# Attention scores kept in DRAM by pairs of heads, in place of a stage of whole tiles in SBUF

## The chip, the cores and the metric

The kernel runs as one program on 1 core of one Trainium2 chip. The metric is device time in microseconds (us). The kernel before takes 1350.86 us (median of 3 runs, 1349.09 to 1351.36).

## The reference

Three layers in float32. The change touches the first alone, an attention whose heads are mixed before and after the softmax:

```python
scores = scale * q @ k.T                                  # 4 batches, 12 heads, 448 queries x 448 keys, D = 64
scores = einsum('bhij,hg->bgij', scores, w_pre)           # mix the heads
attn = softmax(scores, axis=-1)
attn = einsum('bhij,hg->bgij', attn, w_post)              # mix them again
x = (attn @ v)                                            # to [1792, 768]
x = relu(x @ w_in) ** 2 @ w_out                           # feed-forward, 2048 wide
out = gate * relu(x @ w1[e]) @ w2[e]                      # top-1 of 8 experts per token
```

## The kernel before

A matrix multiply can mix heads only if the heads of a query lie on partitions. The scores come out of TensorE the other way, with queries on partitions and one head after another in the free dimension. So all scores (4 x 12 x 448 x 448 floats, 38.5 MB) are moved by DMA from one layout to the other.

**Scores.** `scores(T, j)` (L189) makes one pair of heads `j` for a tile `T` of queries: 6 matmuls (L196; q and k are split into a high and a low part), and a copy by ScalarE (ACT) into `stage[T % 2]` in SBUF (L197), which holds [queries, 12 heads, 448 keys]. A tile has 110 or 118 queries, four tiles a batch, 16 in all. The host has put the queries of a tile in an order in which every G-th row belongs to one group (L1478 to L1482).

**Groups.** A group is 10 queries, taken as 2 halves of 5; 45 groups a batch. `load(p)` (L317) fills the buffer `sg` for the pair of groups `p`, by four DMAs: L328 reads 5 rows of the stage, 12 heads each, and writes 60 partitions of 448 floats. There are four such buffers.

**A tick.** `tick(p)` (L410) is one step of a pipeline with 90 pairs of groups. Its matmuls are the mix of pair p (L343, 8 instructions in the trace: 4 matmuls of two passes each), the second mix of pair p-3 (L375), and in most ticks a piece of attn @ v (`pv`, L395). VectorE (DVE) takes the maximum (L348) and copies results (L384, L399), ACT the exponentials (L354). `make` runs `scores` when `due()` (L304) says so: after a group has been loaded, a target of finished heads for the next tile is noted (L329, L330). The groups of a tile can be loaded only when all its 12 heads are in the stage, and `do_load` (L440) runs LOAD = 2 pairs ahead of the next one.

**Order.** The order of the instructions on each engine is that of the Python program. All DMAs of this phase are issued by SP's one queue, in order: q and k (L174, L183), v once a batch (L302, 1.5 MB), groups (L328), results xT (L401). A DMA that must wait holds up those behind it. After attention comes the feed-forward layer (from L658), whose first weights are loaded in the last ticks (`ahead`, L444; L520, L523).

Of the kernel before, what the change touches and what calls it, by code (L numbers as in the profile page):

```python
# [8 lines left out]
F32 = mybir.dt.float32  # L9
# [13 lines left out]
ROW = 1792  # L23
# [87 lines left out]
        return self.mem.ring(offs, shape, dt) if n else self.mem.at(offs[0], shape, dt)  # L111


def attention(tc, mem, q, k, v, w_pre, w_post, xT, preload, prefetch):

# [3 lines left out]
    nc = tc.nc  # L121
    B, NT, _, HP, MT = q.shape
    S, D, H = k.shape[-1], v.shape[-1], 2 * HP
    NJ = v.shape[2]
    GI = 5
    GP, GC = GI * H, 64
# [1 line left out]
    HH, HQ = H // 2, HP // 2  # L128
    scale = 1.0 / float(D) ** 0.5
    WARM, KEEP = 10, 1  # L130
    LOAD = 2

    with ExitStack() as ctx:
        lo = Cut(mem, Q0, QR + QT + QW)
# [8 lines left out]
        q_raw, raw1, raw2 = lo([128, HP, MT])(), lo([128, S]), lo([128, S])  # L143
        e0 = Cut(mem, E0, 14 * ROW)
        r = Cut(mem, R0, SB_SIZE - R0)
        stage = [c([MT, H, S])() for c in (r, e0)]
        sgs = [c([128, 2, S]) for c in (e0, r, r)] + [mem.at(Q0 + QR + QT, [128, 2, S])]
        e_tiles = [r([128, 8 * GC]) for _ in range(8)]
        e_r = Ring(e_tiles)
# [6 lines left out]
        pairs = mem.open_pairs(ctx)  # L156
        ps_s, ps_o, ps_m = pairs[0], pairs[3], pairs[1:3]

        tiles, groups = [], []
        for b in range(B):  # L160
            for t in range(NT):
                n = S // NT - S // NT % (2 * GI)
                n = S - t * n if t == NT - 1 else n
                G = -(-n // (2 * GI))
                ms = [min(2 * GI, n - 2 * GI * i) for i in range(G)]
                groups += [(len(tiles), i, m) for i, m in enumerate(ms)]
                tiles.append((b, t, G, max(i + G * (m - 1) for i, m in enumerate(ms)) + 1))
        NG, NP = len(groups), len(tiles) * H
        NK, GB = NG // 2, NG // B

        def q_load(T, half):
            b, t = tiles[T][:2]
            c = slice(half * HQ, (half + 1) * HQ)
            nc.sync.dma_start(out=q_raw[:, c], in_=q[b, t][:, c])  # L174

        def q_split(T, half, copy=None):

            c = slice(half * HQ, (half + 1) * HQ)
            (copy or nc.scalar.copy)(q_hi[:, c], q_raw[:, c])
            nc.gpsimd.tensor_tensor(q_lo[:, c], q_raw[:, c], q_hi[:, c].bitcast(F32), ALU.subtract)  # L180
# [4 lines left out]
        def k_split(j, raw, copy=None, eng=None):  # L185
            (copy or nc.scalar.copy)(k_hi[j], raw)
            (eng or nc.gpsimd).tensor_tensor(k_lo[j], raw, k_hi[j].bitcast(F32), ALU.subtract)

        def scores(T, j, ps=ps_s):  # L189

            M = tiles[T][3]
            ps = ps[:M, :, :S]
            for i, (qs, ks) in enumerate(((q_hi, k_hi), (q_lo, k_hi), (q_hi, k_lo))):
                for n in range(2):
                    p = slice(n * D, (n + 1) * D)
                    nc.tensor.matmul(ps[:, n], qs[p, j, :M], ks[j][p], start=(i == 0), stop=(i == 2))  # L196
            nc.scalar.copy(stage[T % 2][:M, 2 * j:2 * j + 2], ps)  # L197

        pro = Cut(mem, A0, SB_SIZE - A0)
        raws = [pro([128, S])() for _ in range(HP)]  # L200
# [27 lines left out]
        for j in range(HP):  # L228
            if j == 1:
                q_split(0, 1, nc.vector.tensor_copy)  # L230
            k_split(j, raws[j], nc.vector.tensor_copy, nc.gpsimd if j in (1, 3) else nc.vector)
            scores(0, j, (ps_s, ps_o)[j % 2])
            keep(KEEP)
        for half in range(2):
            q_load(1, half)
# [4 lines left out]
        for n, (w, src) in enumerate(zip(ws, (w_pre, w_post))):  # L240
            ps = ps_m[1][:, n, :H]
# [4 lines left out]
                nc.vector.tensor_tensor(wpre[:, :GP].rearrange("p (i g) -> p i g", g=H), blk, wr.unsqueeze(1).to_broadcast([128, GI, H]), ALU.mult)  # L246
            else:
                nc.vector.tensor_tensor(wpost, blk.rearrange("p i h -> p h i"), wr.unsqueeze(2).to_broadcast([128, H, GI]), ALU.mult)

        state = {"made": H, "load": 0, "tick": 0}  # L250

        class Feed:

# [5 lines left out]
            def load(self):  # L259
                n = len(self.loaded)  # L260
                self.items[n][1]()
                self.loaded.append(state["tick"])
# [21 lines left out]
        def k_items():  # L284
            place = lambda n: raws3[n % 3]()
            out = []
            for b in range(B - 1):
                for j in range(HP):
                    n = len(out)
                    out.append((("k", b + 1, j), lambda b=b, j=j, n=n: k_load(b + 1, j, place(n)),  # L290
                                lambda j=j, n=n: k_split(j, place(n)),
                                lambda b=b, j=j: state["made"] > ((b + 1) * NT - 1) * H + 2 * j))
            return out
# [1 line left out]
        q_items = [((T, n), lambda T=T, n=n: q_load(T, n), lambda T=T, n=n: q_split(T, n),  # L295
                    lambda T=T, n=n: state["made"] >= (T - 1) * H + (n + 1) * HH) for T in range(len(tiles)) for n in range(2)]
        ks, qs = Feed(k_items(), 3), Feed(q_items, 2, done=4)
        v_t, a_t, sg_t, soft, targets = {}, {}, {}, {}, []

        def v_load(b):  # L300
            v_t[b] = vs()
            nc.sync.dma_start(out=v_t[b], in_=v[b])  # L302

        def due():  # L304

            return (max([n for t, n in targets if t <= state["tick"]] + [state["made"]]) - state["made"]) // 2

        def make(n):

            while state["made"] < min(n, NP):  # L310
                T, h = divmod(state["made"], H)
                qs.need((T, h // HH))
                ks.need(("k", tiles[T][0], h // 2))
                scores(T, h // 2)
                state["made"] += 2

        def load(p):  # L317

            sg_t[p] = sg = sgs[p % 4 if p < NK - 3 else p - NK + 3]()
            for n in range(2):  # L320
                T, i, m = groups[2 * p + n]
                G = tiles[T][2]
                make((T + 1) * H)
                for half in range(2):
                    c = min(GI, m - half * GI)
                    if c > 0:
                        i0 = i + half * GI * G
                        nc.sync.dma_start(out=sg[n * GC:n * GC + c * H, half], in_=stage[T % 2][i0:i0 + G * (c - 1) + 1:G])  # L328
            pace = 1.6 if T + 2 == len(tiles) else 1.25  # L329
            targets.append((state["tick"] + 1, (T + 1) * H + 2 * min(HP, int(HP * pace * (i + 1) / G + 0.5))))  # L330

        def do_load(n):
            while state["load"] < min(2 * n, NG):
# [12 lines left out]
        def row_max(p):  # L346
            soft[p]["nmx"] = nmx_r()
            nc.vector.tensor_reduce(soft[p]["nmx"], soft[p]["ps"][:, :, :S], AX.X, ALU.max, negate=True)  # L348
# [53 lines left out]

            return out

        adds, todo = [], []

        def put(lag, f):
            adds.append((state["tick"] + lag, f))

        def tick(p):  # L410

            state["tick"] += 1
            n = state["tick"]
            ps, ops = ps_m[p % 2], []
            if due() > 1:
                make(state["made"] + 2)
            if todo:
                u, j = todo.pop(0)
                ops.append(pv(u, j, mem.banks[j % 2] if p >= NK + 3 else ps_s[:, j % 2] if state["made"] == NP else ps[:, 0]))
                if j == HP - 1 and (u + 1) * NU % GB == 0 and (u + 1) * NU // GB + 1 < B:  # L420
                    v_load((u + 1) * NU // GB + 1)
            if 0 <= p - 3 < NK:
                ops.append(post(p - 3))
            if 0 <= p - 1 < NK:
                row_max(p - 1)
                exps(p - 1)
            for op in ops:
                op()
            if 0 <= p - 2 < NK:
                scaled(p - 2)  # L430
            if 0 <= p - 3 < NK and any((g + 1) % NU == 0 for g in (2 * p - 6, 2 * p - 5)):
                todo.extend([((2 * p - 5) // NU if (2 * p - 4) % NU == 0 else (2 * p - 6) // NU, j) for j in range(HP)])
            for x in [x for x in adds if x[0] <= n]:
                adds.remove(x)
                x[1]()
            qs.step()
            ks.step()
            if due():
                make(state["made"] + 2)
            do_load(p + 1 + LOAD)  # L440
            if p < NK:
                soft[p] = {"ps": mix(p, ps)}

        ahead = preload(lambda: state["load"] > NG - tiles[-1][2], lambda: state["load"] == NG)  # L444
        for b in range(2):
            v_load(b)
        do_load(1)
# [18 lines left out]
class Ffn:  # L466
# [137 lines left out]
    def preload(self, room, clear):  # L604

        self.rest = self.first_steps(room, clear)
        return self.rest
# [783 lines left out]
def fused_kernel(ctx: ExitStack, tc: tile.TileContext, q, k, v, w_pre, w_post, w_in, w_out, emb, tau, w1, w2, out):  # L1391
    nc = tc.nc
    PE, SP = mybir.EngineType.PE, mybir.EngineType.SP
    H, S = 2 * k.shape[1], k.shape[-1]
    D = v.shape[-1]
    NT, DM = out.shape
    NS = 22
    dram = ctx.enter_context(tc.tile_pool(name="dram", bufs=1, space=DRAM))
    keep = ctx.enter_context(tc.tile_pool(name="keep", bufs=1))
    xT = dram.tile([H * D, NT], F32, name="xT")  # L1400
# [3 lines left out]
    mem = Memory(tc, ctx, SB_SIZE)  # L1404
    en = dram.tile(emb.shape, F32, name="en")
    rt = Router(tc, keep, mem, emb, tau, NT, NS, ident, en)
    ff = Ffn(tc, mem, xT, w_in, w_out, ident, yrow, rt)
# [23 lines left out]
    ET = mybir.EngineType  # L1431
    with tc.manual_schedule(engines={PE}):
        with tc.manual_schedule(engines={SP, ET.Activation, ET.DVE, ET.Pool}):
            attention(tc, mem, q, k, v, w_pre, w_post, xT, ff.preload, ff.prefetch)
        ff.run(late)
    with tc.manual_schedule(engines={PE, SP}):
        wake = ff.last_step(mem.banks[6])
# [2 lines left out]
        rows = ff.tail(mem.bank_ring(2, 3, 4, 5))  # L1440
# [68 lines left out]
```

## Time and profile before

| | us |
|---|---|
| median of 3 runs | 1350.86 |
| profiled execution, its own time | 1344.71 |
| its span (first to last instruction) | 1343.0 |
| PE busy | 1260.3 |
| DVE busy | 934.4 |
| ACT busy | 807.0 |
| POOL busy | 107.0 |

The engines run side by side, so the busy times do not add up. A busy PE is not PE at its peak, since the ends of its pipelined matmuls are modelled. The page's slices show the DMA engines at 3 to 5 tenths during attention; that is a mean over all 16 of them.

### The profile page before, as it was taken

How to read it: one execution, taken by the hardware profiler on the slowest of the kernel's cores; microseconds unless marked ns; L12 is line 12 of the kernel's file. 1: busy time of each engine (PE TensorE's matmuls, PEld its weight loads, DVE VectorE, ACT ScalarE, POOL GpSimd, SP SyncE). 2: the span in 40 equal slices, each digit the busy share in tenths (PEclk: the TensorE clock that was granted, in tenths of full speed). 3: DMA queues.
4: the chain of work that ended last, by engine and by line, in shares of the span. 5: the costliest groups of instructions: out<-in, count | busy, mean ns of one | idle time of the engine just before them, and what ended most of it. 6: DMA issues, size and time to landing. Idle time of an engine off the chain costs nothing. (4 is left out here: it accounts for less than half of the span.)

```text
span 1343.0 us, 31443 instructions
## 1 busy us (share of the span) xinstructions
PE 1260.3 (94%) x12516; PEld 951.2 (71%) x12516; DVE 934.4 (70%) x1598; ACT 807.0 (60%) x1411; POOL 107.0 (8%) x121
## 2 busy tenths in 40 slices
PE   7899979989998869999999999999999999999997
PEld 2455545545655458777898888888886888888886
DVE  3566546655664559998555743498558999999994
ACT  3656545545654546555566444534457888888884
POOL 2020002002000000000000000000001111111100
PEclk7999989998999889999999999999999999999999
DMA  6344344344434545554101000000624147783240
GB/s 219 119 127 145 114 147 143 123 147 126 131 109 121 182 132 176 184 186 155 45 24 60 24 1 0 24 36 12 246 71 178 36 142 280 286 307 115 77 171 26
DMA packets 81641, 166.13 MB, mean 124 GB/s; under 512 B 7359, under 2 KB 58303, under 8 KB 80848
## 3 DMA queue, kind: packets, MB, share of 16 engines
q1 hardware_dynamic: 78432, 151.41, 33.8%
q0 software_dynamic: 2880, 12.59, 2.6%
q8 instruction: 101, 1.65, 0.5%
q14 instruction: 52, 0.43, 0.1%
q10 hardware_dynamic: 176, 0.05, 0.0%
HBM read 184.44 MB, written 18.11 MB: 151 GB/s over the span
## 5 line engine op out<-in xcount | busy, mean ns | idle before, releaser
L577 ACT CAST t<-t 128x768 fp32r<-128x768 f32 x128 | 106.9, 837 | 188.9 <-PE bank L679 84.2
L578 DVE TENSOR_TENSOR t<-t 128x768 fp32r<-128x768 f32 x128 | 122.0, 955 | 120.0 <-ACT t L577 72.1
L343 PE MATMUL pair<-t 60*64 60x448 f32 x720 | 163.7, 595 | 23.4 <-DMA t<-t 22.8
L348 DVE TENSOR_REDUCE t<-pair 128x2 f32<-128x896 f32 x90 | 98.2, 1091 | 102.8 <-PE pair L343 102.7
L354 ACT ACTIVATE t<-pair,t 128x448 f32<-128x448 f32 x180 | 112.5, 631 | 64.0 <-DVE t L348 63.8
L658 PE MATMUL bank<-t 128*128 128x512 f32 (+1 forms) x384 | 140.1, 373 | 8.3 <-ACT t L577 7.3
L1274 DVE TENSOR_TENSOR t<-t 128x768 fp32r<-128x768 f32 x144 | 134.8, 955 | 14.5 <-PE bank L1332 5.0
L384 DVE COPY t<-pair 128x480 f32<-128x480 f32 x168 | 103.0, 652 | 57.4 <-PE pair L375 56.1
L659 PE MATMUL bank<-t 128*128 128x512 f32 (+1 forms) x384 | 138.7, 370 | 1.0 <-DVE t L592 0.9
L1267 DVE TENSOR_TENSOR t<-t 128x1024 fp32r<-128x1024 f32 x102 | 123.3, 1224 | 18.7 <-ACT t L1266 5.3
L197 ACT COPY t<-pair 110x896 f32<-110x896 f32 (+1 forms) x96 | 86.2, 897 | 74.1 <-PE pair L196 37.1
L1273 ACT CAST t<-t 128x768 fp32r<-128x768 f32 x144 | 117.0, 845 | 18.3 <-PE bank L1327 15.3
L1266 ACT CAST t<-t 128x1024 fp32r<-128x1024 f32 x102 | 105.6, 1053 | 25.4 <-PE bank L1289 21.1
L375 PEld LDWEIGHTS pair<-t 60*64 60x64 f32 x5760 | 100.0, 137 | 27.0 <-issue 20.5
L196 PE MATMUL pair<-t 64*110 64x448 f32 (+1 forms) x576 | 89.2, 416 | 26.9 <-ACT t L197 25.3
L375 PE MATMUL pair<-t 60*64 60x60 f32 x5760 | 111.5, 224 | 2.0 <-ACT t L384 1.4
L343 PEld LDWEIGHTS pair<-t 60*64 60x64 f32 x720 | 37.2, 137 | 100.5 <-DMA t<-t 72.3
L395 PEld LDWEIGHTS pair<-t 128*64 128x64 f32 x1056 | 66.9, 142 | 50.4 <-issue 22.9
L1326 PE MATMUL bank<-t 128*128 128x512 f32 (+1 forms) x288 | 98.2, 344 | 0.8 <-ACT t L1337 0.8
L395 PE MATMUL pair<-t 128*64 128x150 f32 (+1 forms) x1056 | 86.2, 308 | 6.4 <-ACT t L399 5.3
L658 PEld LDWEIGHTS bank<-t 128*128 128x128 f32 x384 | 73.9, 192 | 25.2 <-ACT t L577 11.6
L675 PE MATMUL bank<-t 128*128 128x512 f32 (+1 forms) x384 | 90.1, 369 | 0.6 <-ACT t L399 0.6
(219 smaller groups left out, 2312.4 us busy)
## 6 DMA issues: line engine op xcount, KB each, us to landing
t<-in_moe_w_dram SPq DMA_DIRECT2D x120, 512.0 KB
t<-in_moe_w_dram SPq DMA_DIRECT2D x80, 768.0 KB
t<-t SPq DMA_DIRECT2D x356, 105.0 KB
t<-in_moe_w_in_dram SPq DMA_DIRECT2D x16, 768.0 KB
t<-in_moe_w_out_dram SPq DMA_DIRECT2D x16, 768.0 KB
t<-in_vp_dram SPq DMA_DIRECT2D x4, 1536.0 KB
t<-in_q_dram SPq DMA_DIRECT2D x32, 180.0 KB
t<-in_k_dram SPq DMA_DIRECT2D x24, 224.0 KB
```

What stands on the lines that cost most here:

```text
L343: nc.tensor.matmul(ps[half * GC:(half + 1) * GC, n, :S], wpre[i], sg[i, half], start=True, stop=True)
L354: nc.scalar.activation(out=e[:, :S], in_=d["ps"][:, n, :S], func=AF.Exp, bias=d["nmx"][:, n:n + 1], scale=1.0, accum_out=d["z"][:, n:n + 1])
L375: nc.tensor.matmul(wide[c * GC:(c + 1) * GC, r, n, j], e[i, kc * GC:(kc + 1) * GC], wz[i].rearrange("p g i -> p (g i)"), start=True, stop= ...
L395: nc.tensor.matmul(ps[i * D:(i + 1) * D], v_t[u * NU // GB][:, c, h], a_t[u][:, c, h, :n], start=(c == 0), stop=(c == NJ - 1))
L577: nc.scalar.copy(hi, src)
L578: nc.vector.tensor_tensor(lo, src, hi.bitcast(F32), ALU.subtract)
L658: nc.tensor.matmul(ps, wih[:, c], self.xh[k]()[:, :n], start=(k == 0), stop=False)
L659: nc.tensor.matmul(ps, wih[:, c], self.xl[k]()[:, :n], start=False, stop=False)
L1266: nc.scalar.copy(wh, w)
L1267: nc.vector.tensor_tensor(wl, w, wh.bitcast(F32), ALU.subtract)
L1273: nc.scalar.copy(wh, w)
L1274: nc.vector.tensor_tensor(wl, w, wh.bitcast(F32), ALU.subtract)
```

## The change

The stage in SBUF is gone, and with it the order of the queries that the host made. Each `scores` copies its pair of heads into one of 6 small buffers `st` ([112, 2, 448]), and a DMA (L192) writes it to a DRAM tensor `sd[b]` of shape [448 queries, 12 heads, 448 keys], one tick later. A group is loaded from there by one DMA (L326) of 60 partitions x 2 rows. Tiles are now 112 queries throughout. `due(p)` is a straight line in p with a lead of 3 pairs, and DMAs put off to a later tick are issued at the tick's start.

```diff
-        stage = [c([MT, H, S])() for c in (r, e0)]
+        st_r = e0([MT, 2, S], F32, 6)
+        r.off += 12 * ROW
...
+        sd = [dram.tile([S, H, S], F32, name=f"scores{b}") for b in range(B)]
...
-        def scores(T, j, ps=ps_s):
+        def scores(T, j, ps=ps_s, lag=1):
...
-            nc.scalar.copy(stage[T % 2][:M, 2 * j:2 * j + 2], ps)
+            nc.scalar.copy(st, ps)
+            put(lag, lambda: nc.sync.dma_start(out=sd[b][t * MT:(t + 1) * MT, 2 * j:2 * j + 2], in_=st))
...
-            scores(0, j, (ps_s, ps_o)[j % 2])
+            scores(0, j, (ps_s, ps_o)[j % 2], 0)
...
-        def due():
+        def due(p):
-            return (max([n for t, n in targets if t <= state["tick"]] + [state["made"]]) - state["made"]) // 2
+            return min(NP, int((p + LOAD + LEAD) * 4 * GI * H / MT) + H) - state["made"]
...
-                make((T + 1) * H)
-                for half in range(2):
-                    c = min(GI, m - half * GI)
-                    if c > 0:
-                        i0 = i + half * GI * G
-                        nc.sync.dma_start(out=sg[n * GC:n * GC + c * H, half], in_=stage[T % 2][i0:i0 + G * (c - 1) + 1:G])
-            pace = 1.6 if T + 2 == len(tiles) else 1.25
-            targets.append((state["tick"] + 1, (T + 1) * H + 2 * min(HP, int(HP * pace * (i + 1) / G + 0.5))))
+                b, q0, m = groups[2 * p + n]
+                make((b * NT + -(-(q0 + m) // MT)) * H)
+                i = n * GC
+                if m == 2 * GI:
+                    nc.sync.dma_start(out=sg[i:i + GP], in_=sd[b][q0:q0 + m].rearrange("(u c) h s -> (c h) u s", u=2))
+                else:
+                    for u, c in enumerate((GI, m - GI)):
+                        nc.sync.dma_start(out=sg[i:i + c * H, u], in_=sd[b][q0 + u * GI:q0 + u * GI + c].rearrange("c h s -> (c h) s"))
...
+            for x in [x for x in adds if x[0] <= n]:
+                adds.remove(x)
+                x[1]()
-            if due() > 1:
+            if due(p) > 3:
                 make(state["made"] + 2)
...
-            if due():
+            if due(p) > 1:
                 make(state["made"] + 2)
...
-        ahead = preload(lambda: state["load"] > NG - tiles[-1][2], lambda: state["load"] == NG)
+        ahead = preload(lambda: True, lambda: state["load"] == NG)
```

Three places show what moves. The first is SP at the start of the program, before the first mix (`in_vp` is v, `t<-t` a group from the stage):

```order
L208 DMA t<-in_w_post_dram 12x12
L174 DMA t<-in_q_dram 128x360 x2
L302 DMA t<-in_vp_dram 128x3072 x2
L328 DMA t<-t 60x1x448 x4
L174 DMA t<-in_q_dram 128x360
L183 DMA t<-in_k_dram 128x448
L328 DMA t<-t 60x1x448 x8
```

The same place in the changed program (L211 is L208, L169 is L174, L303 is L302):

```order
L211 DMA t<-in_w_post_dram 12x12
L192 DMA scores_110<-t 112x896 x6
L169 DMA t<-in_q_dram 128x336 x2
L303 DMA t<-in_vp_dram 128x3072 x2
L326 DMA t<-scores_110 60x2x448 x2
L169 DMA t<-in_q_dram 128x336
L178 DMA t<-in_k_dram 128x448
L326 DMA t<-scores_110 60x2x448 x4
```

Six writes of scores, each of which waits for ACT's copy, now stand ahead of the loads of q and v. The second place is SP in the middle of attention, before:

```order
L401 DMA xT<-t 128x150
L174 DMA t<-in_q_dram 128x360
L183 DMA t<-in_k_dram 128x448
L328 DMA t<-t 60x1x448 x4
L401 DMA xT<-t 128x150
L183 DMA t<-in_k_dram 128x448
```

And in the changed program (L400 is L401, L178 is L183):

```order
L400 DMA xT<-t 128x150
L192 DMA scores_111<-t 112x896
L169 DMA t<-in_q_dram 128x336
L178 DMA t<-in_k_dram 128x448
L326 DMA t<-scores_111 60x2x448 x2
L400 DMA xT<-t 128x150
L192 DMA scores_111<-t 112x896
```

Per tick, four loads of a group's half became one write and two loads. The third place is PE, from pair 43 on, before (L343 mix, L395 pv, L375 second mix, L196 scores):

```order
L343 MATMUL pair_113<-t 64x448 x4
L395 MATMUL pair_112<-t 64x150 x8
L375 MATMUL pair_114<-t 64x60 x32
L196 MATMUL pair_111<-t 110x448 x6
L343 MATMUL pair_112<-t 64x448 x4
L196 MATMUL pair_111<-t 110x448 x6
L395 MATMUL pair_113<-t 64x150 x8
L375 MATMUL pair_114<-t 64x60 x32
L196 MATMUL pair_111<-t 110x448 x6
L343 MATMUL pair_113<-t 64x448 x4
```

And in the changed program (L342, L394, L374, L190 in their place):

```order
L342 MATMUL pair_107<-t 64x448 x4
L394 MATMUL pair_108<-t 64x150 x8
L374 MATMUL pair_109<-t 64x60 x32
L190 MATMUL pair_106<-t 112x448 x6
L342 MATMUL pair_108<-t 64x448 x4
L394 MATMUL pair_107<-t 64x150 x8
L374 MATMUL pair_109<-t 64x60 x32
```

The scores came in some ticks twice and in others not at all; now nearly each tick has one set, at its end.

## Rows read from the trace of the kernel before

**Rows 1.** Stretches: us; busy of PE, PEld, DVE, ACT, POOL; PEclk, DMA share, GB/s
```profile
0.00:25.70 25.70, 19.38 (x72) 7.29 (x72) 10.69 (x21) 7.63 (x8) 9.07 (x25) 0.82 0.70 246
25.70:425.20 399.50, 359.40 (x6978) 210.99 (x6978) 234.25 (x523) 219.88 (x526) 47.17 (x46) 0.95 0.41 129
425.20:473.70 48.50, 40.75 (x860) 24.40 (x860) 25.90 (x55) 24.19 (x66) 0.00 (x0) 0.93 0.55 172
473.70:510.00 36.30, 25.44 (x361) 21.03 (x361) 24.45 (x40) 18.71 (x41) 0.00 (x0) 0.86 0.52 156
510.00:1343.00 833.00, 815.28 (x4250) 687.49 (x4248) 639.12 (x961) 536.63 (x772) 50.77 (x50) 0.99 0.32 113
```

**Rows 2.** Waits, 25.7 to 473.7: who <- for what: us, times, longest
```profile
PEld pair L343 <- DMA t<-t: 69.4, 81, 5.7
...
PEld pair L196 <- ACT t L197: 41.1, 25, 7.1
...
ACT t L197 <- DMA t<-t: 31.8, 10, 9.9
...
PE pair L343 <- DMA t<-t: 19.4, 30, 5.3
```

**Rows 3.** Timeline of PE, undisturbed stretch: start, us, engine, line, operation, shapes, count
```profile
316.09 0.98 PE L343 MATMUL pair<-t 60*64 60x448 f32 x8
317.00 1.24 PE L395 MATMUL pair<-t 128*64 128x150 f32 x16
318.17 1.16 PE L375 MATMUL pair<-t 60*64 60x60 f32 x64
319.26 0.87 PE L196 MATMUL pair<-t 64*119 64x448 f32 x6
320.06 0.98 PE L343 MATMUL pair<-t 60*64 60x448 f32 x8
...
324.03 0.98 PE L343 MATMUL pair<-t 60*64 60x448 f32 x8
```

**Rows 4.** DMA, 40 to 78 us: packets by size; queue share; issues, KB each
```profile
DMA packets 2709, 4.36 MB, mean 115 GB/s; under 512 B 229, under 2 KB 2701, under 8 KB 2701
...
q1 hardware_dynamic: 2701, 4.25, 35.4%
...
t<-t SPq DMA_DIRECT2D x33, 105.0 KB
t<-in_q_dram SPq DMA_DIRECT2D x4, 180.0 KB
```

**Rows 5.** DMA, 30 to 430 us: the same columns
```profile
DMA packets 35401, 51.51 MB, mean 129 GB/s; under 512 B 3220, under 2 KB 35072, under 8 KB 35072
...
q1 hardware_dynamic: 35328, 50.46, 40.1%
...
t<-t SPq DMA_DIRECT2D x316, 105.0 KB
```

**Rows 6.** SP issue durations, by line: ns min/median/max, first and last start
```profile
L328 SPq DMA_DIRECT2D t<-t x360: 742/763/2046, 16.4 to 465.9; - x180
...
L401 SPq DMA_DIRECT2D xT<-t x72: 319/608/1285, 81.4 to 505.2; - x72
...
L520 SPq DMA_DIRECT2D t<-in_moe_w_in_dram x16: 378/379/1182, 431.1 to 606.4; - x16
```

**Rows 7.** Timeline of the program start, idle time before and its releaser in brackets
```profile
8.13 0.89 SPq L302 DMA_DIRECT2D t<-in_vp_dram  x2
...
15.42 0.91 ACT L197 COPY t<-pair 110x896 f32<-110x896 f32 x1 [0.22 <-PE pair L196]
...
16.35 3.64 SPq L328 DMA_DIRECT2D t<-t  x4
...
20.43 1.72 PE L343 MATMUL pair<-t 60*64 60x448 f32 x2 [2.97 <-DMA t<-t]
```

**Rows 8.** Waits of the SP queue, 30 to 640 us
```profile
SPq L600 <- DMA t<-xT: 8.2, 2, 4.3
```

More of the change, by code (lines that the diff above doesn't have):

```diff
@@ L111, in __call__, with attention @@
         return self.mem.ring(offs, shape, dt) if n else self.mem.at(offs[0], shape, dt)
-def attention(tc, mem, q, k, v, w_pre, w_post, xT, preload, prefetch):
+def attention(tc, mem, dram, q, k, v, w_pre, w_post, xT, preload, prefetch):
     nc = tc.nc
@@ L130, in attention @@
     WARM, KEEP = 10, 1
-    LOAD = 2
+    LOAD, LEAD = 2, 3
     with ExitStack() as ctx:
@@ L157, in attention @@
         ps_s, ps_o, ps_m = pairs[0], pairs[3], pairs[1:3]
[L159 to L167, printed above, removed]
+        tiles = [(b, t) for b in range(B) for t in range(NT)]
+        groups = [(b, q0, min(2 * GI, S - q0)) for b in range(B) for q0 in range(0, S, 2 * GI)]
+        sd = [dram.tile([S, H, S], F32, name=f"scores{b}") for b in range(B)]
         NG, NP = len(groups), len(tiles) * H
@@ L171, in q_load @@
         def q_load(T, half):
-            b, t = tiles[T][:2]
+            b, t = tiles[T]
             c = slice(half * HQ, (half + 1) * HQ)
@@ L187, in k_split @@
             (eng or nc.gpsimd).tensor_tensor(k_lo[j], raw, k_hi[j].bitcast(F32), ALU.subtract)
-        def scores(T, j, ps=ps_s):
-            M = tiles[T][3]
-            ps = ps[:M, :, :S]
+        def scores(T, j, ps=ps_s, lag=1):
+            ps, st, (b, t) = ps[:MT, :, :S], st_r(), tiles[T]
             for i, (qs, ks) in enumerate(((q_hi, k_hi), (q_lo, k_hi), (q_hi, k_lo))):
@@ L195, in scores, with put @@
                     p = slice(n * D, (n + 1) * D)
-                    nc.tensor.matmul(ps[:, n], qs[p, j, :M], ks[j][p], start=(i == 0), stop=(i == 2))
-            nc.scalar.copy(stage[T % 2][:M, 2 * j:2 * j + 2], ps)
+                    nc.tensor.matmul(ps[:, n], qs[p, j], ks[j][p], start=(i == 0), stop=(i == 2))
+            nc.scalar.copy(st, ps)
+            put(lag, lambda: nc.sync.dma_start(out=sd[b][t * MT:(t + 1) * MT, 2 * j:2 * j + 2], in_=st))
+        state, adds = {"made": H, "load": 0, "tick": 0}, []
+        def put(lag, f):
+            if lag:
+                adds.append((state["tick"] + lag, f))
+            else:
+                f()
         pro = Cut(mem, A0, SB_SIZE - A0)
@@ L248, in attention @@
                 nc.vector.tensor_tensor(wpost, blk.rearrange("p i h -> p h i"), wr.unsqueeze(2).to_broadcast([128, H, GI]), ALU.mult)
-        state = {"made": H, "load": 0, "tick": 0}
         class Feed:
@@ L297, in attention @@
         ks, qs = Feed(k_items(), 3), Feed(q_items, 2, done=4)
-        v_t, a_t, sg_t, soft, targets = {}, {}, {}, {}, []
+        v_t, a_t, sg_t, soft = {}, {}, {}, {}
         def v_load(b):
@@ L320, in load @@
             for n in range(2):
-                T, i, m = groups[2 * p + n]
-                G = tiles[T][2]
-                make((T + 1) * H)
-                for half in range(2):
-                    c = min(GI, m - half * GI)
-                    if c > 0:
-                        i0 = i + half * GI * G
-                        nc.sync.dma_start(out=sg[n * GC:n * GC + c * H, half], in_=stage[T % 2][i0:i0 + G * (c - 1) + 1:G])
-            pace = 1.6 if T + 2 == len(tiles) else 1.25
-            targets.append((state["tick"] + 1, (T + 1) * H + 2 * min(HP, int(HP * pace * (i + 1) / G + 0.5))))
+                b, q0, m = groups[2 * p + n]
[3 more added lines that the diff above has]
+                    nc.sync.dma_start(out=sg[i:i + GP], in_=sd[b][q0:q0 + m].rearrange("(u c) h s -> (c h) u s", u=2))
+                else:
+                    for u, c in enumerate((GI, m - GI)):
+                        nc.sync.dma_start(out=sg[i:i + c * H, u], in_=sd[b][q0 + u * GI:q0 + u * GI + c].rearrange("c h s -> (c h) s"))
         def do_load(n):
@@ L403, in pv @@
             return out
-        adds, todo = [], []
-        def put(lag, f):
-            adds.append((state["tick"] + lag, f))
+        todo = []
         def tick(p):
@@ L432, in tick @@
                 todo.extend([((2 * p - 5) // NU if (2 * p - 4) % NU == 0 else (2 * p - 6) // NU, j) for j in range(HP)])
-            for x in [x for x in adds if x[0] <= n]:
-                adds.remove(x)
-                x[1]()
             qs.step()
             ks.step()
-            if due():
+            if due(p) > 1:
                 make(state["made"] + 2)
@@ L1433, in fused_kernel @@
         with tc.manual_schedule(engines={SP, ET.Activation, ET.DVE, ET.Pool}):
-            attention(tc, mem, q, k, v, w_pre, w_post, xT, ff.preload, ff.prefetch)
+            attention(tc, mem, dram, q, k, v, w_pre, w_post, xT, ff.preload, ff.prefetch)
         ff.run(late)
@@ L1477 @@
     k = c(inputs["k"]).transpose(0, 1, 3, 2)
-    qp = np.zeros((B, 4, D, H, 120), np.float32)
-    for t, rows in enumerate((110, 110, 110, 118)):
-        G = -(-rows // 10)
-        for i in range(rows):
-            qp[:, t, :, :, i % 10 * G + i // 10] = q[:, :, :, 110 * t + i]
     vp = np.zeros((B, 512, H, D), np.float32)
@@ L1485 @@
     ins = {
-        "q": c(qp.reshape(B, 4, D, H // 2, 2, 120).transpose(0, 1, 4, 2, 3, 5).reshape(B, 4, 2 * D, H // 2, 120)),
+        "q": c(q.reshape(B, D, H // 2, 2, 4, S // 4).transpose(0, 4, 3, 1, 2, 5).reshape(B, 4, 2 * D, H // 2, S // 4)),
         "k": c(k.reshape(B, H // 2, 2 * D, S)),
```

## The prediction, on record before the changed kernel was run

> **What bounds the kernel now.** I read the stretches first, then the waits of the attention stretch, then an undisturbed piece of PE's timeline, and last the transfers, because the waits point at them.
>
> The stretches cut the span at the end of the first mix (25.7 us), at the 80th (425.2), at the last of the 90 (473.7), and after the hand-over to the feed-forward layer (510) [rows 1]. The change touches the first three. From 25.7 to 425.2 there are 79 ticks in 399.5 us, 5.06 us each. PE counts as busy for 359 of them, but its modelled ends hide waits, so I price a tick from the timeline. In a tick in which nothing is late, the mix starts at 316.09, pv at 317.00, the second mix at 318.17, the scores at 319.26 and the next mix at 320.06; the one after comes at 324.03 [rows 3]. A full tick of PE therefore lasts 3.97 us, and 1.1 us a tick is lost. The waits name the place: the mix waits for the group DMA (69.4 us at the weight loads, in 81 cases, and 19.4 at the matmuls, which overlap these), ACT's copy into the stage waits for group DMAs still reading it (31.8), and the scores wait for that copy (41.1) [rows 2].
>
> Why is the group DMA late, with the DMA engines only 0.41 busy [rows 1]? Between 40 and 78 us just two kinds of transfer were issued, 33 groups and 4 loads of q [rows 4]. The packets under 512 B are not data, whose rows are 1,440 and 1,792 bytes, but what each engine adds when its share of a transfer is done: 229 of them. If the q loads (128 rows) use all 16 engines, 229 - 4 x 16 = 165 remain for 33 groups: 5 engines each. The source of a group is 5 rows of the stage. The rest is arithmetic. The queue moved 4.25 MB in 0.354 x 16 x 38 us, so one engine moves 19.75 GB/s while it works. 33 groups of 107.5 KB over 5 engines take 33 x 107.5 / 5 / 19.75 = 36 us, the q loads spread over 16 take 2.3: these five engines needed 38 of 38 us. The long stretch says the same: 50.46 MB at 19.66 GB/s an engine; 316 groups (34.0 MB) need 346 us of five engines, the other 16.5 MB need 52 of all: 398 of 400 us [rows 5]. A mean share of 0.41 hides five engines that never rest. They bound attention now.
>
> The Trainium skill, page "DMA: Bandwidth & Descriptors", section "Why a DMA increments its semaphore by 16 and not by 1", has a rule for this: a transfer runs on the largest number of engines up to 16 that divides the slowest dimension of both sides. For 5 source rows that is 5, and the trace's count agrees. For the new loads (60 rows on both sides) it would be 15, for the writes (112 rows) 16; a tick of the change would then cost the busiest engine 0.09 us more than the sum below.
>
> **The change part by part.** *Group loads.* The same bytes, 430 KB a tick, now leave DRAM as 60 rows on both sides. No row of before shows a transfer of 60 such rows; the bounds are 5 engines (rows of the old loads) and 16 (128 rows), which give 4.37 and 430 / 16 / 19.66 = 1.37 us a tick on the busiest engine. I take the upper end, since what was few was the 5 rows at the source, and 60 is far nearer to 128 in that.
>
> *Score writes.* New traffic: 401 KB for each of 96 sets, 428 KB a tick, 112 rows, 428 / 16 / 19.66 = 1.36 us. Its rate towards DRAM is bounded by the slowest and the fastest stretch, 156 / (0.52 x 16) = 18.8 and 113 / (0.32 x 16) = 22 GB/s an engine [rows 1]; I keep 19.66. The other transfers stay: 16.5 MB in 400 us, 0.66 us a tick. Sum: 1.37 + 1.36 + 0.66 = 3.39 us a tick on the busiest engine, against 5.06 before. So DMA throughput falls under PE's 3.97, though not far.
>
> *PE, ACT, DVE.* The number of matmuls and copies is unchanged, and rows of a tile (110 or 118, now 112) are partitions, not columns. What changes is when scores are made. Counted in the order, ticks 1 to 79 now hold 51 with one set of scores, pv and second mix, 19 without pv, 9 with two sets (5 of these with pv). Before it was 40 full ones and, up to tick 80, 17 with two sets.
>
> - 51 x 3.97 = 202.5.
> - Without pv, 3.97 - 1.17 (318.17 - 317.00) = 2.80; I take 3.0, since DVE and ACT keep their work: 19 x 3.0 = 57.
> - A second set adds its 0.87 and part of a wait for ACT's copy, since all sets share one pair of PSUM banks; the wait has a mean of 41.1 / 25 = 1.6 us [rows 2, 3], so 0.9 to 2.5; I take 1.2: 5 x 5.17 + 4 x 4.0 = 42.
>
> Together 301 us if nothing is late: 98 less than 399.5. I add 0.4 us a tick, 31 us in all, for what stays late: the engines are then busy 3.39 of 4.2 us on average, v (1.5 MB, 5 us of every engine) comes twice within these ticks, and ticks without pv are shorter than the transfers they order. Its bounds are 0 and the 1.1 us lost now. That leaves 332: a gain of 67.
>
> *SP.* Four loads of 0.76 us a tick become two loads and a write. An issue took 0.32 to 0.76 us, and 768 pieces (L520) cost 0.38, so the number of pieces does not set it [rows 6]. Three issues take 1.0 to 2.3 us, with xT 0.6 and the shares of q and k under 3.5 in all: under a tick, nothing. Writes wait for ACT's copy at the head of the queue, and behind them stand xT, q, k and both loads of pair p+3; they have three ticks, 12 us. The wait of the copy for old readers (31.8) goes: six buffers, one set a tick.
>
> *Start.* The v loads were issued at 8.1, while scores were still being made. Now they stand behind six writes, the last of which waits for the copy that ends at 16.3 [rows 7]. Then 3.1 MB of v (10 us at 16 x 19.66) run ahead of the first groups. Before, the first group was issued at 16.35 and used at 20.43, and the slow five engines stretched the first mix to 25.7. Now I expect it from 27 to 28.5: 3 us lost (0 to 8).
>
> *Last ten ticks.* 48.5 us [rows 1]. No more scores are made there; weights are loaded and converted as before. DMA waits shrink, DVE's conversions do not: 2 us gained (0 to 8). Behind 473.7 nothing changes.
>
> Sum: -67 - 2 + 3 = -66. The profiled execution took 1344.7 us, so 1278.7; the median of the runs is 6.15 above it: 1285.
>
> **The rivals.**
>
> *B: the waits only shrink.* The DMA engines become the bound again, all 16 of them, because reading and writing DRAM at once is slower per packet than what was seen, or because the queue serves bursts badly. For it: 3.39 is 85% of 3.97. Against it: a tick of 4.6 us would need 14.5 GB/s an engine, and no stretch is below 18.8 [rows 1]. At 4.6 us: 79 x 4.6 = 363, a gain of 36, less 3 at the start and with 1 at the end: 1317.
>
> *C: the detour is too long, slower.* At a tile's end a group needs the last set of that tile: copy, write, landing, load, landing. A write of xT to DRAM and the load behind it show the first half: SP waited up to 4.3 us for the landing [rows 8]; a group took 4.1 us from issue to use [rows 7]. With two issues that is 4.3 + 4.1 + 1.5 = 10 us of the 12 that three ticks give, and while SP waits, all loads wait. There are 16 such places. If landings took 1.75 times as long, each place would be 4.3 us late and the gain of 66 gone; at twice as long it is 6.3 x 16 = 101 us: 1386. Against it: these landings were measured behind saturated engines. The same page of the Trainium skill, section "Anatomy of one DMA", speaks for the mechanism: a transfer has a fixed part of about 2 us, mostly the receipt of its write, which is heaviest for DRAM; no row here separates it. By that rule two landings take 4 us, an estimate, less than half of the 8.4 that the rows give.
>
> *D: the spread does not change.* If the new loads, too, used five engines, a tick would need 4.37 + 1.36 + 0.66 = 6.4 us there: 505 us for 79 ticks, 1457.
>
> **How the numbers follow.** Forecast 0.77, B 0.15, C 0.05, D 0.03. Faster by over 0.2% (2.7 us, about what can be told from no change) is the forecast with most of B: 0.90. Within 0.2%: 0.02, B's far end. Slower: 0.08. The range goes from 1258 (nearly all of the 98 us) to 1326 (past B).
>
> **What would show it.** The packets under 512 B per group load: about 16, not 5, with a DMA share of 0.75 or more in attention; a tick of about 4.2 us, most of them 3.97; the waits of mix for DMA under 30 us instead of 69, ACT's wait for DMA gone; the first mix ending at 28 to 29; equal times from the end of attention on. Wrong: if mix still waits in most ticks (B, or D by the packet count), or if SP's waits for a landing stand at the tile ends (C).

## The result, and the profile after

The changed kernel takes 1272.38 us (median of 4 runs, 1270.47 to 1275.38), the kernel before 1349.97 beside it: a ratio of 0.9429, 95% interval [0.9405, 0.9453]. The profiled execution took 1275.38 us, the slowest of its four, and that of before 1344.71, so the two traces differ by 69 us and the medians by 78.

The same stretches, cut at the same events: the end of the first mix, of the 80th, of the last, the hand-over.

```profile
core 0: us, PE busy (x) PEld busy (x) DVE busy (x) ACT busy (x) POOL busy (x), PEclk, DMA share, GB/s
0.00:36.60 36.60, 20.40 (x77) 8.59 (x78) 11.04 (x21) 8.53 (x9) 8.93 (x25) 0.67 0.81 255
36.60:367.70 331.10, 305.50 (x6984) 193.28 (x6984) 232.71 (x523) 217.29 (x527) 45.35 (x46) 0.97 0.87 261
367.70:409.10 41.40, 30.02 (x852) 19.68 (x848) 27.86 (x57) 24.62 (x68) 0.00 (x0) 1.00 0.68 210
409.10:445.40 36.30, 28.54 (x385) 23.79 (x384) 26.27 (x44) 20.31 (x43) 0.00 (x0) 0.95 0.64 193
445.40:1273.60 828.20, 810.25 (x4227) 683.06 (x4225) 634.17 (x954) 533.28 (x768) 51.26 (x50) 0.99 0.32 112
```

Against [rows 1]: the start is 10.9 us longer (36.6 for 25.7), ticks 1 to 79 are 68.4 shorter (331.1 for 399.5), the last ten 7.1 (41.4 for 48.5), all behind attention 4.8 (864.5 for 869.3). DMA went from 129 to 261 GB/s in the long stretch: 1.7 times the bytes in five sixths of the time. PE's granted clock went from 0.95 to 0.97.

What was waited for from the first mix to the end of attention:

```profile
PEld pair L190 <- ACT t L191: 23.1, 20, 2.8
PEld pair L342 <- DMA t<-scores: 9.6, 7, 4.1
ACT t L191 <- DMA scores<-t: 8.1, 1, 8.1
PE pair L342 <- DMA t<-scores: 7.4, 4, 3.7
```

The mix's wait for the group DMA fell from 69.4 us in 81 cases to 9.6 in 7, and ACT's 31.8 in 10 cases to a single one of 8.1 (at the start, below) [rows 2]. The scores' wait for ACT's copy fell less, from 41.1 to 23.1. An undisturbed tick of PE is what it was [rows 3]: mix at 311.74, next mix at 315.71.

```profile
311.74 0.98 PE L342 MATMUL pair<-t 60*64 60x448 f32 x8
...
315.71 0.98 PE L342 MATMUL pair<-t 60*64 60x448 f32 x8
```

The transfers between 30 and 365 us, to set beside [rows 5]:

```profile
DMA packets 47967, 87.42 MB, mean 261 GB/s; under 512 B 5519, under 2 KB 37792, under 8 KB 47627
...
q1 hardware_dynamic: 47894, 86.37, 86.4%
...
scores<-t SPq DMA_DIRECT2D x88, 392.0 KB
t<-scores SPq DMA_DIRECT2D x156, 210.0 KB
```

Take the 5,519 packets under 512 B. If the 88 writes and the 102 other transfers of that stretch (q, k, v, xT and one of weights) use 16 engines each, 2,479 are left for 162 group loads (156 and 6 short ones): 15.3 a load, so 15 engines, not 5. The queue moved 86.37 MB in 0.864 x 16 x 335 us, 18.65 GB/s an engine.

### The profile page after: what moved, and what is told of

It reads as the page before. It is cut to its first block, busy times and chain, and to the rows that moved or that the text cites. A ratio compares the mean times of both kernels' runs of the same rounds, so it can differ in the third digit from the quotient of the medians.

```text
span 1273.6 us, 31397 instructions
## 1 busy us (share of the span) xinstructions
PE 1194.7 (94%) x12515; PEld 928.4 (73%) x12516; DVE 932.0 (73%) x1596; ACT 804.0 (63%) x1413; POOL 105.5 (8%) x121
## 5 line engine op out<-in xcount | busy, mean ns | idle before, releaser
L1270 DVE TENSOR_TENSOR t<-t 128x768 fp32r<-128x768 f32 x144 | 134.9, 955 | 14.4 <-PE bank L1328 5.0
L654 PE MATMUL bank<-t 128*128 128x512 f32 (+1 forms) x384 | 139.0, 370 | 5.9 <-ACT t L573 4.8
L655 PE MATMUL bank<-t 128*128 128x512 f32 (+1 forms) x384 | 137.8, 367 | 1.1 <-DVE t L588 0.8
L1269 ACT CAST t<-t 128x768 fp32r<-128x768 f32 x144 | 116.9, 845 | 18.4 <-PE bank L1323 15.3
L374 PEld LDWEIGHTS pair<-t 60*64 60x64 f32 x5760 | 94.5, 136 | 42.2 <-issue 18.8
L347 DVE TENSOR_REDUCE t<-pair 128x2 f32<-128x896 f32 x90 | 98.1, 1091 | 32.8 <-PE pair L342 32.7
L374 PE MATMUL pair<-t 60*64 60x60 f32 x5760 | 107.1, 222 | 10.9 <-issue 4.2
L191 ACT COPY t<-pair 112x896 f32<-112x896 f32 x96 | 85.8, 894 | 37.9 <-PE pair L190 28.8
L342 PE MATMUL pair<-t 60*64 60x448 f32 x720 | 96.7, 577 | 12.6 <-DMA t<-scores 12.4
L394 PEld LDWEIGHTS pair<-t 128*64 128x64 f32 x1056 | 66.0, 141 | 56.6 <-issue 33.5
L190 PE MATMUL pair<-t 64*112 64x448 f32 x576 | 88.5, 414 | 16.4 <-ACT t L191 14.6
L1322 PE MATMUL bank<-t 128*128 128x512 f32 (+1 forms) x288 | 98.2, 344 | 0.8 <-ACT t L1333 0.8
L394 PE MATMUL pair<-t 128*64 128x150 f32 (+1 forms) x1056 | 85.2, 305 | 10.3 <-ACT t L398 8.6
L671 PE MATMUL bank<-t 128*128 128x512 f32 (+1 forms) x384 | 90.0, 369 | 0.6 <-ACT t L398 0.6
L1323 PE MATMUL bank<-t 128*128 128x512 f32 (+1 forms) x288 | 90.6, 337 | 0.0
```

The lines of the kernel that those rows point to most:

```text
L374: nc.tensor.matmul(wide[c * GC:(c + 1) * GC, r, n, j], e[i, kc * GC:(kc + 1) * GC], wz[i].rearrange("p g i -> p (g i)"), start=True, stop= ...
L394: nc.tensor.matmul(ps[i * D:(i + 1) * D], v_t[u * NU // GB][:, c, h], a_t[u][:, c, h, :n], start=(c == 0), stop=(c == NJ - 1))
L654: nc.tensor.matmul(ps, wih[:, c], self.xh[k]()[:, :n], start=(k == 0), stop=False)
L655: nc.tensor.matmul(ps, wih[:, c], self.xl[k]()[:, :n], start=False, stop=False)
L1269: nc.scalar.copy(wh, w)
L1270: nc.vector.tensor_tensor(wl, w, wh.bitcast(F32), ALU.subtract)
```

## The experiments

Each experiment tests a theory E against a rival, both written down before it ran. Ticks are counted from the end of one mix to the end of the next. In the changed kernel 51 have one set of scores, pv and second mix (median 3.96 us), 19 have no pv (3.29), 5 two sets and pv (6.34).

**Five engines, all else as changed (a1_five).** A dummy thirteenth head in the DRAM tile keeps its rows from joining, so a load walks 5 rows x 12 heads again.

```
-sd = [dram.tile([S, H, S], F32, name=f"scores{b}") for b in range(B)]
+sd = [dram.tile([S, H + 1, S], F32, name=f"scores{b}") for b in range(B)]
...
-nc.sync.dma_start(out=sg[i:i + GP], in_=sd[b][q0:q0 + m].rearrange("(u c) h s -> (c h) u s", u=2))
+for u in range(2):
+    nc.sync.dma_start(out=sg[i:i + GP, u], in_=sd[b][q0 + u * GI:q0 + (u + 1) * GI, :H])
```

> The changed kernel with its group loads put back on five engines: four loads a tick, each from 5 rows x 12 heads of a DRAM tensor padded to 13 heads, so that the two do not merge. Theory E (before, five engines set the pace): loads 430 KB / 5 / 18.65 GB/s = 4.6 us a tick, writes 1.4, the rest 0.7, so 6.7 us a tick on these five, 79 ticks 532 us instead of 331: about 1470. Rival S (what counted was the number of issues on SP, four loads of 0.76 us a tick, and their fixed landing): 3.1 us of loads, write 0.3, xT, q and k 0.9, so 4.3 to 4.7 us a tick: 1290 to 1330.

1373.83 us (1369.03 to 1374.27), 1.0173 [1.0147, 1.0199]: 1.7% slower than before. First the long stretch, then its waits:

```profile
36.50:454.10 417.60, 390.72 (x6985) 223.44 (x6984) 234.85 (x523) 219.88 (x526) 45.33 (x46) 0.94 0.62 206
```

```profile
PEld pair L343 <- DMA t<-scores: 87.7, 116, 4.6
```

The spread over engines is therefore the gain: without it the detour through DRAM costs 24 us. (The loads also doubled in number; the next run takes that part alone. The pad changes the distance between rows in DRAM as well, which was not tried apart.) From 100 to 300 us, at least five packets of the queue were under way at 98% of all moments (82% in before), as they must be if five engines are full.

E's price was too high by 96 us, 1.4 a tick (5.29 us for 6.7). Of this 0.8 are the packets: one of 1,792 B took 79 ns on average (87 in before, where a tenth took over 135; the median is 74 in both), so 48 a tick on each of five engines are 3.80 us, not 4.6. The other 0.6 are open: 1.49 us are left for writes and the rest, where 2.1 had been counted, and spread evenly over 16 engines their packets took that long.

**Two loads for each (a2_split).** The same 15 engines, twice the issues:

```
-nc.sync.dma_start(out=sg[i:i + GP], in_=sd[b][q0:q0 + m].rearrange("(u c) h s -> (c h) u s", u=2))
+for u in range(2):
+    nc.sync.dma_start(out=sg[i:i + GP, u], in_=sd[b][q0 + u * GI:q0 + (u + 1) * GI].rearrange("c h s -> (c h) s"))
```

> The changed kernel with each group load cut into two of 60 rows x 448 floats: four loads a tick as before the change, but from 60 source rows. Theory E: the same bytes on the same engines, SP has time left: 1270 to 1280, no change. Rival S: four issues a tick again, so most of the gain is lost: 1320 to 1350.

1281.88 us (1280.22 to 1288.95), 0.9519 [0.9491, 0.9548]: 0.7% slower than the changed kernel, just past E's range and far from S's. Ticks 1 to 79 took 339.9 us, 8.8 more. So the number of DMAs is worth some 9 us here; with the same number, five engines cost 92 us more (a1_five). It was not what held the kernel before.

**Half the bytes, old kernel (b1_half).** Before, with loads that move 224 of 448 floats; the other half of each score row is left out (zeros).

```
+for g in sgs:
+    nc.gpsimd.memset(g()[:, :, S // 2:], 0.0)
...
-nc.sync.dma_start(out=sg[n * GC:n * GC + c * H, half], in_=stage[T % 2][i0:i0 + G * (c - 1) + 1:G])
+nc.sync.dma_start(out=sg[n * GC:n * GC + c * H, half, :S // 2], in_=stage[T % 2][i0:i0 + G * (c - 1) + 1:G, :, :S // 2])
```

> The kernel before with half of each row left out: every group load moves 224 of 448 floats, the other half of the buffer holds zeros, so the output is not that of the reference. The number of loads, rows, engines and issues stays. Theory E: five engines need 2.2 to 2.7 us a tick for the loads and 0.7 for the rest, under PE's 3.97, so the waits go: 1285 to 1300. Rival S: issues and landings are unchanged: 1340 to 1350.

1316.12 us (1314.4 to 1325.89), 0.978 [0.9746, 0.9814]: by the total, neither. The stretches say more:

```profile
22.70:354.30 331.60, 304.23 (x6979) 192.62 (x6978) 234.46 (x523) 218.28 (x526) 47.21 (x46) 0.99 0.36 104
354.30:392.40 38.10, 31.73 (x862) 20.59 (x860) 25.94 (x56) 24.53 (x67) 0.00 (x0) 1.00 0.55 166
392.40:1312.70 920.30, 881.58 (x4807) 741.94 (x4804) 697.79 (x1038) 586.60 (x854) 56.36 (x54) 0.98 0.34 116
```

Ticks 1 to 79 took 331.6 us, as in the changed kernel, with the old stage, issues and pace; attention ended 81 us earlier. The 51 us given back lie behind it, where PE has 4,807 matmuls instead of 4,609: the routing of the last layer depends on attention's output, so wrong scores can make other work there; that this is the cause of all 51 us was not tried. Bytes on five engines were the limit; E named the right cause, and its gain in attention (50 to 65 us) was too small; S falls.

**The old pace with the new path (a4_old_pace).** The targets of before, in bursts within each tile, in place of the even `due`:

```
...
-            return min(NP, int((p + LOAD + LEAD) * 4 * GI * H / MT) + H) - state["made"]
+            return (max([n for t, n in targets if t <= state["tick"]] + [state["made"]]) - state["made"]) // 2
...
+                if state["sent"] < (b * NT + -(-(q0 + m) // MT)) * H:
+                    while adds:
+                        adds.pop(0)[1]()
```

The last lines issue what was put off at once when a group needs scores not yet sent.

> The changed kernel with the old pace: sets of scores are made in bursts within each tile as before (18 ticks with two sets after the start, 14 of them with pv, instead of 7 and 5), everything else as changed. Theory E (the gain is the spread over 15 engines; the new pace is worth only what double ticks cost): 13 to 20 us slower than the changed kernel, 1286 to 1293 us, so some 60 of its 78 us stay without the new pace. Rival P (the even pace is what hides the transfers, and bursts bring back waits for group loads): 1305 to 1330 us, with the mix waiting for the group DMA over 40 us.

1288.97 us (1288.54 to 1293.31), 0.9554 [0.9536, 0.9571], as E said: 61 of the 78 us stay. Ticks 1 to 79 took 345.5 us, 14.4 more, and two of the waits from 33.7 to 379 are:

```profile
PEld pair L190 <- ACT t L191: 32.1, 23, 2.7
PEld pair L356 <- DMA t<-scores: 14.9, 13, 3.9
```

That is 9 us more behind ACT's copy and 5 more behind the group DMA, whose 14.9 us stand against the 40 and more that P expected.

**The second set out of the pv ticks (c2_doubles).** What such a tick is, from PE's timeline of the changed kernel:

```profile
122.60 0.98 PE L342 MATMUL pair<-t 60*64 60x448 f32 x8
125.09 0.86 PE L190 MATMUL pair<-t 64*112 64x448 f32 x6 [1.51 <-ACT t L191]
125.89 1.24 PE L394 MATMUL pair<-t 128*64 128x150 f32 x16
127.06 1.16 PE L374 MATMUL pair<-t 60*64 60x60 f32 x64
128.15 0.87 PE L190 MATMUL pair<-t 64*112 64x448 f32 x6
128.94 0.98 PE L342 MATMUL pair<-t 60*64 60x448 f32 x8
```

The first set stands right behind the mix, and the set before the mix has not yet been copied out of the one pair of banks: 3.96 + 0.87 + 1.51 = 6.34 us.

```
-if due(p) > 3:
+more = due(p) > (3 if todo else 2)
+if more:
...
-if due(p) > 1:
+if more or due(p) > -2:
```

> The changed kernel with another pace: the five ticks with two sets of scores and pv (6.3 us each) are gone; their second set stands in a tick without pv. Theory E (such a tick waits for ACT's copy between its two sets, while PE has nothing else): 56 ticks of 3.96, and seven without pv and two sets at about 4.5; 5 x (6.3 + 3.3 - 4.0 - 4.5) = 6 us gained, 1266 to 1268 us. Rival R (the second set is worth its PE time wherever it stands): no change, 1271 to 1274 us.

1266.09 us (1265.17 to 1271.71), 0.9385 [0.9364, 0.9406]: 6 us below the changed kernel, inside E's range, but in part by luck. 56 ticks have a median of 3.96 and none has two sets and pv; ticks 1 to 79 took 325.0 us for 331.1. A second set without pv costs more than E said, 5.17 us a tick, not 4.5, and with that E's sum is 5 x (6.34 + 3.29 - 3.96 - 5.17) = 2.5 us. Part of the rest is not the pace's: tick 33, behind a v load (see c1_pieces), took 4.71 us in this trace and 9.18 in that of the changed kernel, and tick 55 0.8 us more.

**v first (a3_early_v).** The first two v loads right behind those of k and the weights, ahead of the six score writes:

```
...
+for b in range(2):
+    v_load(b)
 rep = pro([H, 2, GC])()
```

> The changed kernel with the first two loads of v issued right behind those of k and the mixing weights, ahead of the six score writes. Theory E for the start (3.1 MB of v run ahead of the first groups): the first mix ends at 27 to 29 us instead of 36.6, 8 us gained: 1264. Rival R (the first mix waits for the way through DRAM, write, landing, load): it ends at 35 to 37 as now: 1272.

1274.02 us (1268.65 to 1278.53), 0.9441 [0.9414, 0.9468]: no difference. The first mix ends at 32.8 instead of 36.6, and E's 27 to 29 is missed. Even these 3.8 us are hardly the edit's: a2_split and a4_old_pace, in which v still stands behind the writes, end theirs at 33.0 and 33.7, and like this run they had a granted clock of 1.00 from 8 to 16 us, where the changed kernel's trace has 0.57. What held the mix here was q:

```profile
24.79 1.50 DVE L174 CAST t<-t 128x336 fp32r<-128x336 f32 x2 [12.44 <-DMA t<-in_q_dram]
26.57 0.60 PE L253 MATMUL pair<-t 12*128 12x12 f32 x2 [12.14 <-DVE t L255]
30.99 1.77 PE L346 MATMUL pair<-t 60*64 60x448 f32 x8
```

From 8 to 20 us the DMA engines are 0.98 to 1.00 busy, and q's next two loads stand behind v and the writes. DVE waits for them before it makes the mixing weights (L255), PE waits for DVE, and after two sets of scores the mix starts without any wait for a group. With 3.1 MB of v ahead of q (here) or ahead of the first groups (the changed kernel), the mix is late either way.

**v behind the groups, in pieces (c1_pieces).** In the changed kernel the start goes like this, SP's issues first:

```profile
16.59 1.53 SPq L192 DMA_DIRECT2D scores<-t  x2
18.21 1.11 SPq L169 DMA_DIRECT2D t<-in_q_dram  x2
19.37 0.98 SPq L303 DMA_DIRECT2D t<-in_vp_dram  x2
22.28 1.07 SPq L326 DMA_DIRECT2D t<-scores  x2
...
25.28 8.16 SPq L326 DMA_DIRECT2D t<-scores  x4
```

```profile
33.98 2.58 PE L342 MATMUL pair<-t 60*64 60x448 f32 x8 [5.00 <-DMA t<-scores]
```

Both v loads go out at 19.4, the first groups at 22.3 behind them, the mix starts 11.7 us after that, and the next four loads need 8.16 us to be issued (in them SP waits for v's transfer, 6.5 us in two cases); a score write stands behind them, which is ACT's one wait of 8.1. Two more v loads, in ticks 33 and 55 (9.18 and 8.55 us long), do the same to the groups behind them:

```profile
166.34 0.85 PE L190 MATMUL pair<-t 64*112 64x448 f32 x6
169.42 1.72 PE L342 MATMUL pair<-t 60*64 60x448 f32 x2 [2.23 <-DMA t<-scores]
```

```
...
+                nc.sync.dma_start(out=v_t[b][:, c], in_=v[b][:, c])
...
+            for c in range(NJ):
+                put(first + 2 * c, lambda c=c: piece(c))
...
+        do_load(1)
         for b in range(2):
-            v_load(b)
-        do_load(1)
+            v_load(b, 1 + 2 * NJ * b)
```

> The changed kernel, but every load of v (1.5 MB) is cut into four of 393 KB, one every second tick, and the first two v loads start behind the first groups instead of ahead of them. Theory E (the start and the two long ticks are group loads queued behind a whole v load): first mix ends at 28 to 31 instead of 36.6; ticks 33 and 55 fall from 9.2 and 8.6 us to about 4.5; together 1257 to 1264 us. Rival R (the 16 engines are the limit anyway at a share of 0.87, so the same bytes come late in other ticks): the first mix is earlier but ticks 1 to 16 get longer by as much, 1269 to 1276 us.

1260.97 us (1260.33 to 1268.37), 0.9362 [0.9337, 0.9386], as E said. SP, DVE, PE and the stretches of this kernel:

```profile
14.73 0.30 SPq L192 DMA_DIRECT2D scores<-t  x1
15.13 2.36 SPq L169 DMA_DIRECT2D t<-in_q_dram  x2
19.04 0.82 SPq L331 DMA_DIRECT2D t<-scores  x2
19.91 0.40 SPq L305 DMA_DIRECT2D t<-in_vp_dram  x1
```

```profile
19.54 1.50 DVE L174 CAST t<-t 128x336 fp32r<-128x336 f32 x2 [7.22 <-DMA t<-in_q_dram]
25.75 1.77 PE L347 MATMUL pair<-t 60*64 60x448 f32 x8
```

```profile
0.00:27.50 27.50, 16.49 (x78) 7.16 (x78) 11.17 (x21) 8.54 (x9) 8.81 (x25) 0.83 0.78 236
27.50:351.60 324.10, 300.69 (x6987) 192.96 (x6984) 233.08 (x523) 217.64 (x527) 45.46 (x46) 0.99 0.91 275
```

The first mix ends at 27.5, and ticks 33 and 55 last 3.96 and 3.05. Of the 9.1 us at the start some 3 go with the clock, from 8 to 16 us 0.57 in the changed kernel's trace and 1.00 here: with 1.00 and the changed kernel's order, a2_split and a4_old_pace came to 33.0 and 33.7. The other 6 are the order of the queue. The mix no longer waits for a group; ahead of it stand q, for which DVE waits up to 19.5, and two sets of scores.

In the ticks the DMA engines moved 275 GB/s, and the mix waited 5.9 us for its groups at its weight loads; the changed kernel had 261 and 9.6. So its share of 0.87 was not their limit.

**A shorter lead (c3_lead2).**

```
-LOAD, LEAD = 2, 3
+LOAD, LEAD = 2, 2
```

> The changed kernel with the scores made one tick later (a lead of two ticks, some 8 us, instead of three, 12 us); the rest is as changed, but for one tick with two sets less with pv. It prices the detour through DRAM (copy, write, landing, load, landing), which the prediction put at 10 us at each of 16 tile ends. Theory C (10 us is right): each of these places is 2 us late, 32 us in all, 1300 to 1310 us, and SP waits for the landing of scores 2 us and more at tile ends. Theory E (the detour is shorter than 8 us once the engines are not saturated): 1266 to 1276 us, SP's waits for the landing of scores below 15 us in all.

1273.32 us (1265.08 to 1274.24), 0.9416 [0.9391, 0.9441]: no difference, as E said. But E's sign is missed and C's is there. The waits from 36 to 410 us, of SP for the landing of scores and of the mix for its group:

```profile
SPq L326 <- DMA scores<-t: 33.2, 14, 4.4
```

```profile
PEld pair L342 <- DMA t<-scores: 4.5, 9, 1.6
```

E had allowed SP 15 us in all; in the changed kernel it is 5.4 us in 4 cases. So with two ticks the scores are often not yet in DRAM when SP wants them, 2.4 us on average. SP stands, and yet the mix hardly waits. That it is the two pairs loaded ahead that cover this was not tried.

**Both gains (c5_both).** c1_pieces with the pace of c2_doubles.

> The v loads in pieces and behind the first groups, and the pace without double ticks with pv, together. Theory E: the two gains add, 1251 to 1259 us, faster than both kernels. Rival R (DMA is the limit at the start and in the ticks): 1267 to 1273 us.

1258.08 us (1257.34 to 1263.88), 0.9335 [0.9314, 0.9356]: faster than both kernels, by 14 us than the changed one, and at the slow end of E's range. The gains add only in part, 14 of 11 + 6: on top of c1_pieces the pace gives 2.9 us, which lies within the spread of the two runs and near the 2.5 worked out for it under c2_doubles.

```profile
0.00:28.70 28.70, 17.93 (x78) 7.60 (x78) 11.05 (x21) 8.54 (x9) 8.94 (x25) 0.75 0.75 223
28.70:350.90 322.20, 302.42 (x6988) 193.73 (x6984) 232.98 (x523) 217.53 (x527) 45.49 (x46) 0.97 0.91 277
```

## Why the prediction was right

- *The bound.* Five engines, read off the small packets [rows 4, 5]: shown from two sides. Fewer bytes on them (b1_half) free the ticks, and five engines in the new path (a1_five) bind them again. "Never rest" was a little strong: fewer than five packets were under way for 18% of the time.
- *The spread.* 16 engines a load were taken; the trace has 15.3 small packets a load. The rule cited from the Trainium skill (page "DMA: Bandwidth & Descriptors", section "Why a DMA increments its semaphore by 16 and not by 1") gives 15 for 60 rows; the trace agrees, with 15.3. The 0.09 us a tick between the two decide nothing. The sum of 3.39 us a tick came out as 0.87 x 331.1 / 79 = 3.65, mostly since an engine moved 18.65 GB/s, not 19.66; it stayed under PE's 3.97.
- *Ticks 1 to 79.* 332 us predicted, 331.1 measured, but the 31 us of allowance were right in size and wrong in kind. They were put down to late transfers in all ticks. In truth full ticks stand at 3.96, and the 30 us are the doubles (52.4 us with pv and without, where 42 was counted: with pv the set and a wait of 1.51 behind the copy, 2.4 in all, not 1.2), the ticks without pv (a median of 3.29, not 3.0), and the two ticks behind a v load (some 10 us together).
- *The pace.* The prediction did not price it apart. It is worth 14 us in the ticks and 17 in the total (a4_old_pace). It is no fixed price of the bursts: b1_half, with bursts and half the bytes, took 331.6 us for the same ticks.
- *Start: the term that was mis-sized.* +3 us predicted, 0 to 8 as bounds; +10.9 measured. The step saw v's 10 us ahead of the first groups, yet let the first mix end at 27 to 28.5. It counted no time for the issues in between (v went out at 19.4, after the sixth write at 18 and q) and let the first groups land as v ended. And it left out that q's loads, too, now stand behind the six writes: DVE waits for q up to 22.8 us before it makes the mixing weights, and two sets of scores (one before) stand between these and the mix. With v out of the way the first mix ends 1.8 us later than before (c1_pieces, clock 1.00 from 8 to 16 us) or 3.0 (c5_both, 0.79, as before): that is what is left of the detour, and in c1_pieces it is q, not a group, that the mix waits for. The other 8 to 9 us are v's place in the queue, some 6, and the clock. Loads of q ahead of the writes were not tried.
- *Last ten ticks and behind.* -2 predicted (0 to 8), -7.1 measured: in bounds, and the half-size loads of b1_half (38.1 us) say that these ticks, too, waited for the five engines more than was counted. Behind attention -4.8 where 0 was said; the traces of a1, a2, a3, a4, c1, c2, c3 and c5 hold 863.0 to 869.2 us there, with the same work and no pattern that follows the edits, so nothing is claimed for it.
- *The rivals.* B (16 engines bind) falls with c1_pieces: more bytes a microsecond, less waiting. C (the detour is too long) was priced at 10 us a place, and with a lead of 8 its sign came, SP waiting 14 times for 2.4 us on average; its cost did not, since the mix waited 4.5 us in all (c3_lead2). So a wait of SP does not by itself make the mix late. The section of the Trainium skill that was named for C ("Anatomy of one DMA") is headed for transfers that GpSimd issues; here SP issues them, and no run shows the fixed part by itself. D (five engines), forced in a1_five, comes to 1374 us, not 1457: a packet of 1,792 B at 19.66 GB/s takes 91 ns, and 79 were measured, 0.6 of the 1.1 us by which a tick came out shorter (5.29 for 6.4); the rest is open, as said there.
- *The sum.* -66 us predicted, -69.4 between the profiled executions. That it fits so well is partly luck: the start was 7.9 us worse than said, the last ten ticks and what lies behind them 9.9 better. The median came 12.6 us below the forecast, mostly since the forecast added the 6.15 us by which the median of before lay above its profiled execution, and that of after lies 3.0 below.

## What to carry to other kernels

A low mean DMA share can hide a few engines that are full: divide the small packets by the transfers, then the bytes by that number of engines. When a limit goes, the next ones are single events (a large transfer ahead of small urgent ones, two sets of scores in a row on one pair of banks), which a uniform allowance prices right only by luck; list them by length of tick and move them. Where later work depends on the data, judge an experiment that leaves data out by its stretches, never by its total.

## What was not expected of the hardware

- Packets of 896 B took 41 ns (median) and of 1,792 B 74: 33 ns for the second half, so by these two little of a packet's time is fixed (some 8 ns, an estimate).
- The same 1,792-byte packets averaged 87 ns in before (nearly all out of SBUF) and 79 out of DRAM in a1_five, both with five engines full, and 91 out of DRAM in the changed kernel, all at the same median of 74; what makes the long ones was not tried.
- A wait can cost PE more than its length. Two places of the changed kernel's trace, ticks 33 and 37, each cut at the wait and behind it:

```profile
164.20:173.40 9.20, 6.55 (x96) 3.03 (x98) 3.12 (x7) 4.22 (x10) 3.12 (x3) 0.78 0.94 297
173.40:178.00 4.60, 4.60 (x90) 3.58 (x94) 2.39 (x4) 1.34 (x4) 0.00 (x0) 0.69 0.96 258
...
187.60:191.00 3.40, 1.42 (x8) 0.82 (x10) 1.18 (x2) 2.08 (x5) 1.99 (x2) 0.83 0.94 269
191.00:196.00 5.00, 5.00 (x96) 3.40 (x96) 1.93 (x6) 2.09 (x6) 0.00 (x0) 0.77 0.92 262
```

PE stood 2.65 us in the first and was busy 1.42 of 3.40 us in the third; in both the granted clock fell from full speed, and behind them, with PE busy throughout, it was 0.69 and 0.77 on average, a mix of its two levels (1.2 and 2.4 GHz). Tick 34, with nothing late, took 5.30 us for 3.96. Tick 37 took 8.36 where its like took 6.34 at full clock, and its wait was only 0.48 us longer (1.99 for 1.51). The v load of tick 33 and this one of the five doubles so cost more than their waits.
